# Chunked attention and two FFNs: token pairs of 512 and 384 columns, weight factors in two tiles, all attention weights transposed by TensorE

## The chip, the cores and the metric

The kernel runs on one core of one Trainium2 chip. The metric is the device time in microseconds (us) of one execution; less is better. TensorE (PE) multiplies, VectorE (DVE), ScalarE (ACT) and GpSimd (POOL) do the elementwise work, SyncE (SP) issues every DMA of this kernel. The weight loads of PE are shown as an engine of their own, PEld.

## The reference

Everything is float32. Attention works on chunks of 64 tokens; its output, 4608 tokens of 512 channels, goes through two feed-forward layers of 512 to 2048 to 512.

```python
scores = scale * np.matmul(q_c, k_c.transpose(0, 1, 2, 4, 3))   # chunks of 64, 8 batches, 8 heads, head size 64
scores = scores - np.max(scores, axis=-1, keepdims=True)
attn = np.exp(scores)
attn = attn / (np.sum(attn, axis=-1, keepdims=True) + 1e-09)
x = np.matmul(attn, v_c)                     # then put together as (4608, 512)
h = x @ w_in1
x = (h / (1.0 + np.exp(-1.702 * h))) @ w_out1
h = x @ w_in2
out = (np.maximum(h, 0.0) + alpha * np.minimum(h, 0.0)) @ w_out2
```

The weights arrive as 64-bit floats and are decoded on the chip by integer operations on VectorE.

## The kernel before, in words

Each float32 operand of a large product is split in a rounded part ("hi") and the rest ("lo"), and three matmuls (hi hi, hi lo, lo hi) make one product. A matmul has a stationary operand of 128x128, loaded by a weight load of its own, and a moving operand of up to 512 columns (tokens).

**First layer.** There are 9 blocks of 512 tokens and 16 slots f in each block, slot number n = 16 block + f. A slot runs `emit_h` (L446): 12 matmuls of 512 columns into a bank psH (there are two of them), a sigmoid on ACT (L460), then the work that `middle()` inserts, then the product g by DVE (L462), which frees the bank, and the split of g into gs by ACT (L117) and by DVE or POOL (L120). Then comes `emit_y` (L469) for the slot before last: 12 matmuls of 512 columns into the four psY. In slot 15 of a block x is split for the next block (`split_x`, L425). All engines run their own instructions in order, and the order is the order of the program text; nothing is reordered.

Attention of the later blocks is fitted between these. Each group g of 128 tokens from g = 4 on (four groups a block) has steps at half slots relative to 8 (g - 4): -4 `att_T` (transposes of q and k, L306), -1 `att_S` (scores, row maximum, difference, L332) and `att_E` (exponential on ACT, sum and reciprocal on DVE, the product e on POOL, L366), +2 `att_AT` (L372), +5 `att_PV` (product with v, two copies of x by ACT, L417). An even half slot is run in `middle()`, an odd one after `emit_y`. `att_AT` transposes e. Up to g = 7 TensorE does it, four transposes into a PSUM bank and one copy by ACT (L382, L387); from g = 8 on, 28 groups, DVE does it in 16 instructions of 32x128 each (L392). The banks come from `psum_att`, a pool of two that the scores, the transposes and the two banks of `att_PV` share in turn.

q and k of a group are loaded in 8 parts of several DMAs each (`load_qk`, L284), two groups ahead; v of the next group is loaded at half slot +5 into one of two buffers.

The second layer's weights are prepared in the same time, in 32 steps from slot 18 on, 3.25 slots apart (lists `todo`, key "prep"). A step, in slots from its base slot: +1 `prep_load` (raw weights), +2 `prep_abs` (Abs on ACT, L149), +3 `prep_decode` (four DVE operations), +4 `prep_store_a` (cast by ACT L222 and subtraction by POOL L223 into the tile "st2", store of 3 quarters by L205, then four sums on POOL), +6 `prep_store_b` (the same for the sums, into the same tile, all 4 quarters).

**Second layer.** Each matrix product is done with seven products of half-size blocks in place of eight. Tokens are taken in pairs: `PAIRS` has five entries, and a pair of n columns covers 2n tokens. For each pair there are four groups gr of hidden units; each has seven H products i in the order `H_ORDER`, of 2 x 6 matmuls of n columns each (L647), and seven Y products of 12 matmuls (L759) in `Y_ORDER`. H uses two bank pairs, psHa (i = 1, 6, 7, 4) and psHb (2, 5, 3); products are summed in the bank where they can be, and DVE and ACT take the rest (`h_after`, L674: copies, sums L692, `relus` L660, `leak` L665). Y uses psYa and psYb likewise and adds into `yacc` by DVE (L777) or ACT (L775).

The order is written by hand: a slot has one H product and one Y product of the group before, and a clock counts 1 for each half of an H product and 2 for a Y product. `at(when, ...)` puts work due at a clock value. `plan_group` (L721) sets when the Y operands are made: `op_hi` (ACT, L706), `op_lo` (DVE, L711), and the four differences (`diff`, L716, on POOL, in the last group on DVE). The first Y product comes when the first eight H products are done, so no Y product lies between the first group's H products. Weights are read from DRAM for every pair into rings of nine tiles (`load_wi`, L577) and four tiles (`load_wo`, L586), each reload issued when a tile has been used. `y_out` (L784) and, for the last pair, `y_last` (L799) transpose and store the output.

Of the kernel before, what the change touches and what calls it, by code (L numbers as in the profile page):

```python
# [9 lines left out]
F32 = mybir.dt.float32  # L10
# [23 lines left out]
PAIRS = (480, 480, 448, 448, 448)  # L34

H_ORDER = (1, 2, 6, 5, 7, 3, 4)
Y_ORDER = (1, 5, 6, 3, 7, 2, 4)
# [8 lines left out]
def tile_chunk_attention_two_ffn(  # L46
# [173 lines left out]
    def prep_split(step, src):  # L220
        t = prep_p.tile([P, 4, 2, P], F32R, tag="st2", name="st2")
        nc.scalar.copy(t[:, :, 0], src)  # L222
        nc.gpsimd.tensor_tensor(out=t[:, :, 1], in0=src, in1=t[:, :, 0].bitcast(F32), op=ALU.subtract)  # L223
        return t

    def prep_store_a(step):
        u = pr[step]
        t = prep_split(step, u)
        prep_store(step, 0, 3, t[:, 0:3])
        sums = dec_p.tile([P, 4, P], F32, tag="u", name="sums")  # L230
        a11, a12, a22, a21 = (u[:, q] for q in range(4))
        for o, x, y, op in (
            (0, a21, a22, ALU.add), (1, sums[:, 0], a11, ALU.subtract),
            (2, a11, a21, ALU.subtract), (3, a12, sums[:, 1], ALU.subtract),
        ):
            nc.gpsimd.tensor_tensor(out=sums[:, o], in0=x, in1=y, op=op)
        pr[step] = sums

    def prep_store_b(step):
        t = prep_split(step, pr.pop(step))  # L240
        prep_store(step, 3, 7, t)
# [20 lines left out]
    def load_qkv(g, names="qkv"):  # L262

        for nm in names:
            if g < GPB:
                t = {
                    "q": lambda: spare(f"wi{NF - GPB + g}", 0),
                    "k": lambda: spare(f"wi{NF - GPB + g}", 1),
                    "v": lambda: spare(f"wo{NF - 1 - g // 2}", g % 2),
                }[nm]()  # L270
            else:
                t = qkv_p.tile([P, 512], F32, tag=nm, name=nm, bufs=2)
# [99 lines left out]
    def att_AT(g):  # L372
# [5 lines left out]

        if g < 2 * GPB:
            ps = psum_att("psAT")  # L380
            for hp in range(HP):
                nc.tensor.transpose(  # L382
                    ps[:, hp * P:(hp + 1) * P],
                    e[:, 2 * hp:2 * hp + 2, :].rearrange("p u t -> p (u t)"),
                    ident,
                )
            nc.scalar.copy(t.rearrange("p h t -> p (h t)"), ps)  # L387
        else:
            blocks = e.rearrange("p (h c) (b e) -> p h c b e", c=2, e=SQ)
            for i in range(P // SQ):  # L390
                for o in range(P // SQ):
                    nc.vector.transpose(  # L392
                        t[o * SQ:(o + 1) * SQ, :, i * SQ:(i + 1) * SQ],
                        blocks[i * SQ:(i + 1) * SQ, :, o // 2, o % 2, :],
                    )
# [176 lines left out]
    hs = [(p, gr, i, jj) for p in range(NP) for gr in range(NGR) for i in H_ORDER for jj in range(2)]  # L572
# [22 lines left out]
    def second_layer():  # L595
# [125 lines left out]
        def plan_group(p, gr, u):  # L721

            n = PAIRS[p]
            last = (p, gr) == (NP - 1, NGR - 1)
            times = (23, 25, 27, 30, 35, 39, 43) if last else (27, 30, 34, 36, 44, 46, 49)
# [6 lines left out]
            t1, t2, t3, t4 = (24, 26, 29, 30) if last else (24, 32, 29, 38)  # L732
# [126 lines left out]
    with tc.manual_schedule():  # L859
# [50 lines left out]
        for i, step in enumerate(steps):  # L910
            n = PREP_FROM + int(i * PREP_EVERY)
            for lag, fn in enumerate((None, prep_load, prep_abs, prep_decode, prep_store_a, None, prep_store_b)):
                if fn:
                    todo.setdefault(("prep", n + lag), []).append(partial(fn, step))
# [3 lines left out]
        for g in range(GPB, NG):  # L918
# [3 lines left out]
            if g + 1 < NG:  # L922
                between[8 * (g - GPB) + 5].append((load_v, g + 1))
# [9 lines left out]
        for n in range(NBLK * NF):  # L933
# [14 lines left out]
            emit_h(n, middle, nc.gpsimd if ("decode", n) in todo else nc.vector)  # L948

# [60 lines left out]
```

## Time and profile before

| | us |
|---|---|
| three timed runs | 1734.43, 1737.24, 1738.43 |
| median | 1737.24 |
| the profiled execution's own time | 1733.37 |
| its span | 1731.6 |

The profile is of one execution. Rows of a timeline or chain give the start and the length, then engine, line and operation, out<-in by tile names, shapes and how many were merged (x12); a bracket gives the idle time before and what ended it. A merged matmul row also holds the last one's way through the array; the chain's lengths run to the next row's start.

### The profile page before, as it was taken

The page shows a single profiled execution, that of the slowest core. Times are in us where ns is not written, and L with a number is a line of the kernel's source. Part 1 is how long each engine was busy: PE and PEld are TensorE (multiplying, and loading weights), DVE is VectorE, ACT ScalarE, POOL GpSimd, SP SyncE. Part 2 cuts the span into 40 slices and gives each one's busy share as a digit, 9 for nine tenths or more (in the row PEclk, how much of TensorE's full clock was granted, in tenths as well). Part 3 has the DMA queues.
Part 4 walks back from the last instruction along what each step waited for, and adds up shares of the span by engine and source line. Part 5 has one row for each costly group of instructions (what it writes and reads, how often), then busy time and mean ns, then how long its engine had stood idle before and what let it go on. Part 6 is the DMA issues. An engine that isn't in the chain of part 4 may idle for free.

```text
span 1731.6 us, 25761 instructions
## 1 busy us (share of the span) xinstructions
PE 1631.3 (94%) x9257; PEld 1366.9 (79%) x9259; DVE 1267.8 (73%) x1858; ACT 785.2 (45%) x1098; POOL 500.4 (29%) x382
## 2 busy tenths in 40 slices
PE   7879998999988999989999989999999999999997
PEld 5667876777767777767788878888888998998996
DVE  7998666686666777757774347887788788788776
ACT  5554434344334443434433344555455455554542
POOL 3664122222212222212222024223422423422320
PEclk9999999999999999999999999999999999999999
DMA  8741334444334344334423067669667877977854
GB/s 229 215 115 36 73 88 110 114 109 111 93 92 107 107 110 115 101 97 118 100 62 125 0 214 249 203 180 293 214 204 194 309 217 193 313 212 192 278 180 121
DMA packets 388591, 268.11 MB, mean 155 GB/s; under 512 B 265840, under 2 KB 328048, under 8 KB 388464
## 3 DMA queue, kind: packets, MB, share of 16 engines
q1 hardware_dynamic: 388464, 266.47, 53.8%
q8 instruction: 73, 1.20, 0.3%
q14 instruction: 54, 0.44, 0.1%
HBM read 218.11 MB, written 48.23 MB: 154 GB/s over the span
## 4 chain that ended last, share of the span: by engine, by line
PE 45%; DVE 19%; DMA 8%; SPq 8%; ACT 7%; issue 4%; POOL 2%; DVEq 0%; ACTq 0%; POOLq 0%
PE psYa L759 10%; PE psHa L647 9%; PE psYb L759 7%; PE psHb L647 6%; SPq L297 6%; PE psH L453 6%; PE psY L476 5%; DMA raw<-in_moe_w_in_dram 3%; DMA raw<-in_moe_w_out_dram 3%; DVE g L462 2%; DVE g L666 2%; DVE at L392 2%; ACT gs L117 2%; DVE gs L120 1%; DVE o L711 1%
## 5 line engine op out<-in xcount | busy, mean ns | idle before, releaser
L453 PE MATMUL psH<-xs,wi 128*128 128x512 f32 x1728 | 442.7, 407 | 33.1 <-DVE g L462 29.5
L453 PEld LDWEIGHTS psH<-xs,wi 128*128 128x128 f32 x1728 | 330.6, 195 | 113.6 <-DVE g L462 37.8
L476 PE MATMUL psY<-gs,wo 128*128 128x512 f32 x1728 | 415.1, 390 | 3.6 <-ACT gs L117 3.6
L476 PEld LDWEIGHTS psY<-gs,wo 128*128 128x128 f32 x1728 | 323.7, 188 | 73.2 <-ACT gs L117 5.5
L117 ACT CAST gs<-g 128x512 fp32r<-128x512 f32 x144 | 89.3, 620 | 351.6 <-DVE g L462 351.6
L759 PE MATMUL psYa<-o,w 128*128 128x448 f32 (+1 forms) x960 | 218.6, 376 | 6.3 <-ACT o L706 3.8
L647 PE MATMUL psHa<-xop,wi2t 128*128 128x448 f32 (+1 forms) x960 | 216.0, 374 | 4.8 <-ACT g L663 4.4
L759 PEld LDWEIGHTS psYa<-o,w 128*128 128x128 f32 x960 | 180.2, 189 | 32.1 <-ACT o L706 5.1
L647 PEld LDWEIGHTS psHa<-xop,wi2t 128*128 128x128 f32 x960 | 181.7, 189 | 26.6 <-ACT g L663 4.8
L462 DVE TENSOR_TENSOR g<-psH,g 128x512 f32<-128x512 f32 x144 | 98.4, 683 | 138.5 <-ACT g L460 137.7
L666 DVE SCALAR_TENSOR_TENSOR g<-neg,minus_alpha,g 128x448 f32<-128x448 f32 (+1 forms) x160 | 182.7, 1182 | 6.8 <-ACT g L663 6.7
L759 PE MATMUL psYb<-o,w 128*128 128x448 f32 (+1 forms) x720 | 161.9, 373 | 0.0
L647 PE MATMUL psHb<-xop,wi2t 128*128 128x448 f32 (+1 forms) x720 | 160.1, 371 | 0.0
L120 DVE TENSOR_TENSOR gs<-g,gs 128x512 fp32r<-128x512 f32 x129 | 93.7, 726 | 88.6 <-ACT gs L117 87.9
L716 POOL TENSOR_TENSOR tsum<-g,tsum 128x896 f32<-128x896 f32 (+1 forms) x39 | 92.6, 2375 | 199.7 <-DVE o L711 196.9
L759 PEld LDWEIGHTS psYb<-o,w 128*128 128x128 f32 x720 | 134.8, 188 | 16.9 <-DVE o L711 0.6
L647 PEld LDWEIGHTS psHb<-xop,wi2t 128*128 128x128 f32 x720 | 135.2, 188 | 15.4
L716 POOL TENSOR_TENSOR tsum<-g,g 128x896 f32<-128x896 f32 (+1 forms) x19 | 41.6, 2188 | 350.9 <-DVE g L666 301.9
L392 DVE STREAM_TRANSPOSE at<-e 32x128 f32<-32x128 f32 x448 | 135.5, 302 | 6.7
L662 ACT ACTIVATE neg<-g 128x896 f32<-128x896 f32 (+1 forms) x60 | 58.5, 975 | 124.1 <-DVE g L692 124.1
L460 ACT ACTIVATE g<-psH 128x512 f32<-128x512 f32 x144 | 85.8, 596 | 50.7 <-PE psH L453 50.3
L711 DVE TENSOR_TENSOR o<-tsum,o 128x896 fp32r<-128x896 f32 (+1 forms) x60 | 66.5, 1109 | 46.1 <-ACT o L706 44.0
(117 smaller groups left out, 1898.8 us busy)
## 6 DMA issues: line engine op xcount, KB each, us to landing
wi2t<-wi SPq DMA_DIRECT2D x280, 256.0 KB, 3.8
w<-wo SPq DMA_DIRECT2D x140, 512.0 KB, 3.6
x<-ysb SPq DMA_DIRECT2D x36, 256.0 KB, 2.5
raw<-in_moe_w_in_dram SPq DMA_DIRECT2D x16, 512.0 KB, 5.4
raw<-in_moe_w_out_dram SPq DMA_DIRECT2D x16, 512.0 KB, 4.3
raw<-in_moe_w_in_dram SPq DMA_DIRECT2D x32, 256.0 KB, 3.9
wi<-st SPq DMA_DIRECT2D x16, 512.0 KB, 2.9
raw<-in_moe_w_out_dram SPq DMA_DIRECT2D x32, 256.0 KB, 3.5
```

The lines of the kernel that those rows point to most:

```text
L117: nc.scalar.copy(hi, src)
L120: eng_lo.tensor_tensor(out=lo, in0=src, in1=hi.bitcast(F32), op=ALU.subtract)
L297: nc.sync.dma_start(out=t[r:r + SQ, h // 2, off // SQ:(off + n) // SQ], in_=src[b, h, s:s + n, y * SQ:(y + 1) * SQ].rearrange("(b t) e -> ...
L392: nc.vector.transpose(t[o * SQ:(o + 1) * SQ, :, i * SQ:(i + 1) * SQ], blocks[i * SQ:(i + 1) * SQ, :, o // 2, o % 2, :],)
L453: nc.tensor.matmul(ps, w[:, a, c], xs[:, b, c], start=(i == 0), stop=(i == 3 * KT - 1))
L460: nc.scalar.activation(out=g, in_=ps, func=AF.Sigmoid, scale=1.702)
L462: nc.vector.tensor_tensor(out=g, in0=ps, in1=g, op=ALU.mult)
L476: nc.tensor.matmul(y_t[j][t], w[:, a, t * P:(t + 1) * P], gs[:, b], start=(f == 0 and a + b == 0), stop=(f == NF - 1 and b == 1),)
L647: nc.tensor.matmul(ps, w[:, c, a], x[b][:, c], start=(k == 0 and i in (1, 2, 5)), stop=(k == 5 and i in (2, 3, 4)), skip_group_check=True,)
L666: nc.vector.scalar_tensor_tensor(out=g, in0=neg, scalar=minus_alpha[:, f:f + 1], in1=g, op0=ALU.mult, op1=ALU.add)
L716: eng.tensor_tensor(out=wide(homes[out], n), in0=wide(homes[x], n), in1=wide(homes[y], n), op=ALU.subtract,)
L759: nc.tensor.matmul(ps[:, d, :n], w[:, jj, d, a], x[b][:, jj], start=(k == 0 and i in (1, 5, 2)), stop=(k == 5 and i in (3, 2, 4)), skip_gr ...
```

## The change

The pairs become three of 512 and two of 384 columns (2304 in all, as before). The first group (pair 0, gr 0) takes its H products in the order `H_FIRST`, with 4 before 3, and the last one in `H_LAST`, with 5 before 6 and 3 before 7; `plan_group` has other due times for the first, the last but one and the last group. The prepared factors go to two tiles, "sta" for 3 quarters and "stb" for 4, and the first cast and subtraction treat 3 quarters only; Abs is issued behind `emit_h` of the slot +3 (key "abs"), and `prep_store_b` at +5. TensorE transposes e for all groups. v has one buffer from g = 4 on, and its load stands at half slot +7.

```diff
--- before.py
+++ after.py
@@ -31,9 +31,12 @@
 PREP_FROM = 18
 PREP_EVERY = 3.25
 
-PAIRS = (480, 480, 448, 448, 448)
+PAIRS = (512, 512, 512, 384, 384)
 
 H_ORDER = (1, 2, 6, 5, 7, 3, 4)
+
+H_FIRST = (1, 2, 6, 5, 7, 4, 3)
+H_LAST = (1, 2, 5, 6, 3, 7, 4)
 Y_ORDER = (1, 5, 6, 3, 7, 2, 4)
 PLACE = {1: 0, 2: 1, 3: 6, 4: 2, 5: 3, 6: 4, 7: 5}
 
@@ -217,16 +220,15 @@
         except StopIteration as done:
             pr[step] = done.value[0].rearrange("p (q f) -> p q f", q=4)
 
-    def prep_split(step, src):
-        t = prep_p.tile([P, 4, 2, P], F32R, tag="st2", name="st2")
+    def prep_split(src, n, tag):
+        t = prep_p.tile([P, n, 2, P], F32R, tag=tag, name=tag)
         nc.scalar.copy(t[:, :, 0], src)
         nc.gpsimd.tensor_tensor(out=t[:, :, 1], in0=src, in1=t[:, :, 0].bitcast(F32), op=ALU.subtract)
         return t
 
     def prep_store_a(step):
         u = pr[step]
-        t = prep_split(step, u)
-        prep_store(step, 0, 3, t[:, 0:3])
+        prep_store(step, 0, 3, prep_split(u[:, 0:3], 3, "sta"))
         sums = dec_p.tile([P, 4, P], F32, tag="u", name="sums")
         a11, a12, a22, a21 = (u[:, q] for q in range(4))
         for o, x, y, op in (
@@ -237,8 +239,7 @@
         pr[step] = sums
 
     def prep_store_b(step):
-        t = prep_split(step, pr.pop(step))
-        prep_store(step, 3, 7, t)
+        prep_store(step, 3, 7, prep_split(pr.pop(step), 4, "stb"))
 
 
     def spans(t0, n):
@@ -269,7 +270,7 @@
                     "v": lambda: spare(f"wo{NF - 1 - g // 2}", g % 2),
                 }[nm]()
             else:
-                t = qkv_p.tile([P, 512], F32, tag=nm, name=nm, bufs=2)
+                t = qkv_p.tile([P, 512], F32, tag=nm, name=nm, bufs=1 if nm == "v" else 2)
             t = t.rearrange("p (h d) -> p h d", h=H)
             for off, n, b, s in spans(g * P, P):
                 nc.sync.dma_start(
@@ -375,24 +376,14 @@
             t = spare(f"wi{NF - GPB - 1 - g % 2}", 1).rearrange("p (h t) -> p h t", h=HP)
         else:
             t = at_p.tile([P, HP, P], F32, tag="at", name="at")
-
-        if g < 2 * GPB:
-            ps = psum_att("psAT")
-            for hp in range(HP):
-                nc.tensor.transpose(
-                    ps[:, hp * P:(hp + 1) * P],
-                    e[:, 2 * hp:2 * hp + 2, :].rearrange("p u t -> p (u t)"),
-                    ident,
-                )
-            nc.scalar.copy(t.rearrange("p h t -> p (h t)"), ps)
-        else:
-            blocks = e.rearrange("p (h c) (b e) -> p h c b e", c=2, e=SQ)
-            for i in range(P // SQ):
-                for o in range(P // SQ):
-                    nc.vector.transpose(
-                        t[o * SQ:(o + 1) * SQ, :, i * SQ:(i + 1) * SQ],
-                        blocks[i * SQ:(i + 1) * SQ, :, o // 2, o % 2, :],
-                    )
+        ps = psum_att("psAT")
+        for hp in range(HP):
+            nc.tensor.transpose(
+                ps[:, hp * P:(hp + 1) * P],
+                e[:, 2 * hp:2 * hp + 2, :].rearrange("p u t -> p (u t)"),
+                ident,
+            )
+        nc.scalar.copy(t.rearrange("p h t -> p (h t)"), ps)
         at_t[g] = t
 
     x_t = {}
@@ -569,7 +560,12 @@
 
 
 
-    hs = [(p, gr, i, jj) for p in range(NP) for gr in range(NGR) for i in H_ORDER for jj in range(2)]
+    FIRST_G, LAST_G = (0, 0), (NP - 1, NGR - 1)
+    h_order = {FIRST_G: H_FIRST, LAST_G: H_LAST}
+    hs = [
+        (p, gr, i, jj) for p in range(NP) for gr in range(NGR)
+        for i in h_order.get((p, gr), H_ORDER) for jj in range(2)
+    ]
     ys = [(p, gr, i) for p in range(NP) for gr in range(NGR) for i in Y_ORDER]
     wi_order, wo_order, wi_q, wo_q = list(hs), list(ys), [], []
     turn = {"wi": 0, "wo": 0}
@@ -721,15 +717,20 @@
         def plan_group(p, gr, u):
 
             n = PAIRS[p]
-            last = (p, gr) == (NP - 1, NGR - 1)
-            times = (23, 25, 27, 30, 35, 39, 43) if last else (27, 30, 34, 36, 44, 46, 49)
+            last = (p, gr) == LAST_G
+            times = {
+                FIRST_G: (27, 31, 36, 37, 44, 46, 49), LAST_G: (23, 22, 26, 28, 34, 38, 42),
+                (NP - 1, NGR - 2): (27, 30, 34, 33, 44, 46, 40),
+            }.get((p, gr), (27, 30, 34, 36, 44, 46, 49))
             for i, nm, hi in zip(
                 (1, 5, 6, 3, 7, 2, 4), ("g11", "t", "t", "g22", "t3", "g21", "t"), times
             ):
                 at(u + hi, op_hi, p, gr, i, nm)
                 at(u + hi + 1, op_lo, p, gr, i, nm)
             eng = nc.vector if last else nc.gpsimd
-            t1, t2, t3, t4 = (24, 26, 29, 30) if last else (24, 32, 29, 38)
+            t1, t2, t3, t4 = {FIRST_G: (28, 34, 30, 38), LAST_G: (20, 24, 28, 29)}.get(
+                (p, gr), (24, 32, 29, 38)
+            )
             at(u + t1, diff, n, "t", "g12", "g11", eng)
             at(u + t2, diff, n, "t", "g22", "t", eng)
             at(u + t3, diff, n, "t3", "g22", "g12", eng)
@@ -909,9 +910,11 @@
         ]
         for i, step in enumerate(steps):
             n = PREP_FROM + int(i * PREP_EVERY)
-            for lag, fn in enumerate((None, prep_load, prep_abs, prep_decode, prep_store_a, None, prep_store_b)):
-                if fn:
-                    todo.setdefault(("prep", n + lag), []).append(partial(fn, step))
+            for what, lag, fn in (
+                ("prep", 1, prep_load), ("abs", 3, prep_abs), ("prep", 3, prep_decode),
+                ("prep", 4, prep_store_a), ("prep", 5, prep_store_b),
+            ):
+                todo.setdefault((what, n + lag), []).append(partial(fn, step))
 
 
         between = {}
@@ -920,7 +923,7 @@
                 if g > GPB or at > 0:
                     between.setdefault(8 * (g - GPB) + at, []).append((fn, g))
             if g + 1 < NG:
-                between[8 * (g - GPB) + 5].append((load_v, g + 1))
+                between.setdefault(8 * (g - GPB) + 7, []).append((load_v, g + 1))
             if g + 2 < NG:
                 for part in range(8):
                     between.setdefault(max(0, 8 * (g - GPB) - 1 + part), []).append(
@@ -946,6 +949,8 @@
                 dec = ahead
 
             emit_h(n, middle, nc.gpsimd if ("decode", n) in todo else nc.vector)
+            for fn in todo.get(("abs", n), []):
+                fn()
 
 
             ahead_y = {0: (n - 1,), 1: (), NF - 1: (n - 2, n - 1)}.get(f, (n - 2,))
```

## Rows read from the trace of the kernel before

**Rows 1.** the page's first line: span and instruction count

```profile
span 1731.6 us, 25761 instructions
```

**Rows 2.** chain in order of time, first layer: start us, us, what

```profile
162.09 2.95 PE psH L453 x12
176.54 2.95 PE psH L453 x12
200.46 2.95 PE psH L453 x12
...
907.97 2.72 PE psH L453 x12
```

**Rows 3.** waits, 162 to 908 us: who waited for whom, us, times, longest

```profile
ACT u L149 <- DMA raw<-in_moe_w_in_dram: 41.5, 13, 6.0
ACT u L149 <- DMA raw<-in_moe_w_out_dram: 41.1, 14, 5.0
PEld psH L453 <- DVE g L462: 25.4, 24, 4.0
PEld psS L340 <- ACT x L417: 18.1, 11, 4.1
PEld psX L409 <- DVE at L392: 16.0, 18, 2.3
ACT st L222 <- DMA wi<-st: 9.1, 4, 6.1
```

**Rows 4.** timeline of ACT and PE, 494 to 526 us: start, us, what

```profile
504.07 0.66 ACT L149 ACTIVATE u<-raw 128x512 f32<-128x512 f32 x1 [5.97 <-DMA raw<-in_moe_w_in_dram]
520.60 0.62 ACT L222 CAST st<-u 128x512 fp32r<-128x512 f32 x1 [6.09 <-DMA wi<-st]
...
523.91 2.45 PE L453 MATMUL psH<-xs,wi 128*128 128x512 f32 x5 [3.24 <-DVE g L462]
```

**Rows 5.** groups by line, attention's transposes: busy us, mean ns | idle before

```profile
L392 DVE STREAM_TRANSPOSE at<-e 32x128 f32<-32x128 f32 x448 | 135.5, 302 | 6.7
L387 ACT COPY at<-psAT 128x512 f32<-128x512 f32 x4 | 2.3, 574 | 0.0
```

**Rows 6.** timeline of PE's weight loads at 138 us, four transposes by TensorE

```profile
138.50 0.56 PEld L382 LDWEIGHTS psAT<-ident,e 128*128 128x128 f32 x4
```

**Rows 7.** timeline of PE and POOL at 515 us

```profile
515.07 2.88 PE L453 MATMUL psH<-xs,wi 128*128 128x512 f32 x12
...
515.81 1.05 POOL L366 TENSOR_TENSOR e<-e,d 128x512 f32<-128x512 f32 x1 [6.55 <-DVE d L365]
```

**Rows 8.** chain in order of time: matmuls of 512, 480 and 448 columns

```profile
989.57 8.16 PE psY L476 x36
1033.89 2.62 PE psYb L759 x12
1036.52 2.59 PE psHb L647 x12
...
1706.14 2.48 PE psYb L759 x12
1716.93 2.44 PE psYb L759 x12
```

**Rows 9.** timeline of weight loads after a pause; their group by line

```profile
1460.67 0.30 PEld L759 LDWEIGHTS psYa<-o,w 128*128 128x128 f32 x2 [0.80 <-DVE o L711]
...
L759 PEld LDWEIGHTS psYa<-o,w 128*128 128x128 f32 x960 | 180.2, 189 | 32.1 <-ACT o L706 5.1 <-DVE o L711 4.2 <-issue 1.2
```

**Rows 10.** timelines of PE and DVE at the second layer's start and end

```profile
1021.05 5.01 PE L647 MATMUL psHa<-xop,wi2t 128*128 128x480 f32 x12 [4.43 <-ACT g L663]
...
1702.15 3.99 PE L759 MATMUL psYa<-o,w 128*128 128x448 f32 x12 [3.84 <-ACT o L706]
...
1700.90 1.15 DVE L777 TENSOR_TENSOR yacc<-psYa,yacc 128x448 f32<-128x448 f32 x2
```

**Rows 11.** busy us by stretch: PE, PEld, DVE, ACT, POOL; clock, DMA share, GB/s

```profile
1454.00:1489.00 35.00, 34.24 (x166) 30.76 (x165) 26.52 (x29) 17.61 (x20) 11.11 (x6) 1.00 0.92 258
```

## The prediction

> **What bounds the kernel now.** I read the page first: the span is 1731.6 us [rows 1] and the profiled execution took 1733.37 us. The median of the three timed runs, 1737.24, lies 3.9 us above it. Then the chain in order of time splits the span. In the first layer the reader is to see an undisturbed stretch: a psH group starts at 176.54 and the one four slots later at 200.46, so four slots with one attention group in them take 23.92 us [rows 2]. Sixteen slots (a block) should then take 95.7 us and seven blocks 669.8 us. The seven blocks from 162.09 to 907.97 took 745.9 us [rows 2]. So TensorE, in order, loses 76 us there, and the waits name the losses [rows 3]: psH for VectorE's L462 25.4, scores for ScalarE's copies of x 18.1, the attention's product psX for VectorE's transposes L392 16.0, some 60 us of the 76. I put most of the rest down to the halved clock that follows such pauses.
>
> Two waits of ScalarE stand behind the first two of these. Its Abs of the second layer's raw weights (L149) waits 82.6 us for their load, and its cast into the tile "st2" (L222) waits for the store of the tile's earlier content [rows 3]. In [rows 4] one of each is seen, 5.97 and 6.09 us, and psH stands still for 3.24 us at 523.91, just behind the second.
>
> In the second layer TensorE is nearly gapless, so the time of one matmul counts. The rows give 8.16 us for 36 of 512 columns, 226.7 ns each; 2.62 and 2.59 us for 12 of 480, about 217; 2.48 and 2.44 us for 12 of 448, 206.7 and 203.3 [rows 8]. I take 205 for 448. Two pauses stand out: 4.43 us after the first group, then 12 matmuls in 5.01 us instead of 2.6, as at the lower clock level, 1.2 GHz, and 3.84 us ahead of the last group's products, then 3.99 instead of 2.48 [rows 10].
>
> **The change, part by part.**
>
> *Transposes.* For 28 groups it removes 448 VectorE transposes, 135.5 us [rows 5], and adds 112 TensorE transposes and 28 ScalarE copies at 574 ns, 16.1 us of ScalarE. The four transposes of an earlier group held the weight loads for 0.56 us [rows 6]; part of that lies under the matmuls around it, so I take 0.5 us a group, 14 us on the path. The wait for L392 goes whole: the copy now follows TensorE directly and the product comes three half slots later. TensorE now waits for e itself, in order, with the next psY group queued behind. In [rows 7] GpSimd ends e at 516.86 and TensorE ends the matmuls ahead of the transposes at 517.8, so I cost this wait at nothing, 0.9 us being the cover. VectorE's L462 no longer queues behind 4.8 us of transposes. Late next would be the block boundary, where L462 queues behind the split of x.
>
> *Abs, two tiles, v.* Abs moves from the end of a slot to behind the next slot's gs cast, about half a slot of two 2.72 us groups later, and behind one more sigmoid, so a wait of 6 us at most [rows 3] should shrink to little. The load of raw weights keeps its place on SP's queue. Two tiles let a cast run while the other tile's store is out. The first cast and subtraction lose a quarter of their columns, off the path. The b store moves a slot earlier on SP, and may hold the next q and k loads, which are two groups ahead. With one buffer for v, its load, moved two half slots later, waits for the product of the group before; queued behind on SP are q and k pieces and the raw loads. No row prices it: between nothing and half a slot now and then. I take nothing, because the v is needed six half slots later.
>
> Together: the 16.0 us go. Of the 43.5 us of the other two waits I take half, 22, because the block boundary and SP's many small loads remain. With some 6 us of half clock this removes 44. The bounds are the 16 alone and all 76. Net of 14: 30 us gained, between 2 and 62.
>
> *Columns.* The number of matmuls and the sum of columns stay; only their split moves. A pair is 672 matmuls (4 groups, 7 products, 24 each). Before: 1344 at 217.5 and 2016 at 205 ns, 705.6 us. After: 2016 at 226.7, 457.0 us, and 1344 of 384 columns, which no row shows. Over the stream itself (columns at 2.4 GHz, the full level) the rows leave 13.4 ns at 512, 17.5 at 480, 18.3 at 448. For 384, 160 ns of stream, I take 19, as at 448, the nearest: 179 ns, 240.6 us. That is 697.6, 8 us less. The lower bound is 13.4 ns over the stream, 173.4 ns, 16 us less; the upper bound is no gain over 448, 205 ns, 275.5 us, 27 us more. A constant cost per matmul would make the split worth exactly nothing, since columns and count are unchanged; what the 8 us rest on is that 512 pays least. The Trainium skill, "TensorE: Matmul & The Clock Gate", section "Back-to-back issue gap", has such a constant, columns at 2.4 GHz plus 2.5 ns; by it the term is 0. The rows' 13.4 to 18.3 ns are larger and not constant, so I go by them, and keep 0 as a rival.
>
> *First and last group.* In the first group product 4 comes before 3, so ScalarE's two passes over bank a run beside product 3's 2.7 us. New is that 4 follows 7 in the same bank and waits for VectorE's addition; the bank's addition of the last group, 1.15 us [rows 10], is the nearest row, so 1.5 us with the way there and back. Of 4.43 plus the 2.4 us of slow matmuls, 5 go (bounds 2 and 7). At the end, bank psYa came free only with VectorE's addition ending at 1702.05 [rows 10], queued behind the last group's differences. The new order and times issue these some clock steps earlier; what stays is the addition itself, 1.15 us. Of 3.84 plus 1.5 us I take 4 (bounds 0 and 5). The other shifted times of the last but one group I cost at nothing, hidden by TensorE's row of products.
>
> *Sum.* 1733.4 - 30 - 8 - 5 - 4 = 1686.4 for an execution like the profiled one. The median stands 3.9 above; taking half of that, I say 1688.
>
> **Rivals.**
>
> *Constant cost per matmul.* As above: 1696.
>
> *Weight transfers.* Each pair reads the same weights, and shorter pairs read them faster. One stretch of 35 us, about a group of 448 columns, has a DMA share of 0.92, 32.2 us of transfers [rows 11]; a 384 group (168 matmuls at 179 ns) is 30 us. Nine and four tiles of read-ahead, over half a group, cover one such stretch. Where they do not, each group waits 2.2 us, in the four groups of a pair 9 us: 1697.
>
> *No relief in the first layer.* SP's many loads or the block boundary take up what VectorE and ScalarE give. Only the 16 us go, against 14: 1716. For it speaks that the raw load is late because of SP, which is not relieved; against it that Abs is given half a slot.
>
> *384 no faster than 448.* If a matmul cannot follow a weight load faster than now, the price is 205 ns: 35 us over my forecast, 1723. Against it: after a pause two weight loads lie in 0.30 us, where one takes 189 ns on average [rows 9], so the second began some 0.11 us after the first, and 160 ns leave room. The Trainium skill, same page, section "LDWEIGHTS (loading the stationary operand)", gives columns over 1.2, 107 ns for 128; the trace's 0.11 us agrees.
>
> *Slower: TensorE waits for e.* The transposes stand in TensorE's own queue, ahead of the psY group. With stalls gone TensorE reaches them sooner, while e's way (maximum, exponential, sum, product on three engines) does not shorten. The price is 28 times the wait. It decides from 49 us over my forecast, 1.75 us a group; at 2.2 us a group it gives 62 more, 1750. Against it is the 0.9 us to spare at a stalled place [rows 7].
>
> **How the numbers follow.** My forecast 0.45, constant cost 0.12, transfers 0.06, no relief 0.17, flat 384 0.11, waits for e 0.09. The likeliest gives 1688. Downward, all of the 76 less some, with the lower column bound, reaches 1664; upward the range takes in no relief and a little of flat 384, to 1722. A measurement of this kernel tells about 0.2%, 3.5 us, from no change. The slower cases are waits for e, and flat 384 without relief, 1751: 0.10. Between, 0.03. Faster 0.87.
>
> **What would show it.** The blocks of the first layer at 98 to 103 us instead of 106.6; no L392; psX's wait gone; L149's wait for raw below 30 us; no L222 wait; four transposes holding 0.5 us a group; psAT's wait for e below 10 us in all. In the second layer 12 matmuls of 512 in 2.72 us and of 384 in 2.08 to 2.2; the first pause about 1.5 us, the last about 1.2. The prediction is wrong if 12 of 384 take 2.4 us, if psAT waits over 1 us a group, or if blocks stay above 105 us.

## Result and profile after

The changed kernel takes 1690.78 us (median of four runs, 1689.83 to 1691.14), beside 1737.84 for the kernel before in the same comparison (four runs; the table ahead has three of them). The ratio is 0.973 with an interval of 0.971 to 0.975: 2.7% faster. The forecast was 1688 in a range of 1664 to 1722. The profiled execution took 1690.86 us; its span follows, where [rows 1] had 1731.6.

```profile
span 1689.1 us, 25576 instructions
```

Two stretches split the span, and I use them for every run below. **Seven blocks** run from the first psH group of the second block to that of the ninth: 745.8 us before, 705.0 after. The **second layer** runs from its first matmul to the end: 734.0 before (997.6 to 1731.6), 733.3 after (955.7 to 1689.1). So nearly all of the gain of the span (42.5 us) lies in the first layer, 40.8 where 30 were forecast, and the second layer gave 0.7 where 17 were. The stretches are those of one profiled execution of each kernel.

**First layer.** From the chain in order of time, as in [rows 2]; start and length in us:

```profile
176.00 2.95 PE psH L444 x12
...
200.42 2.95 PE psH L444 x12
```

Four undisturbed slots now take 24.42 us instead of 23.92. The half microsecond is the four transposes on TensorE; the weight loads of one such group, from PE's timeline as in [rows 6], and ScalarE's copies, from the groups by line as in [rows 5]:

```profile
190.75 0.59 PEld L381 LDWEIGHTS psAT<-ident,e 128*128 128x128 f32 x4
```

```profile
L386 ACT COPY at<-psAT 128x512 f32<-128x512 f32 x32 | 18.6, 582 | 0.0
```

Twenty-eight groups of 24.42 us are 684 us, so of the seven blocks 21 us are pauses. Before it was 76 (745.8 less 669.8). The waits of the seven blocks, as in [rows 3]: who waited for whom, us in total, times, longest:

```profile
ACT u L152 <- DMA raw<-in_moe_w_in_dram: 32.0, 7, 11.8
ACT u L152 <- DMA raw<-in_moe_w_out_dram: 23.6, 6, 10.6
...
PEld psS L341 <- ACT x L408: 12.3, 5, 4.4
...
PE psS L341 <- ACT x L408: 10.2, 3, 4.0
...
PE psX L400 <- DMA v<-in_v_dram: 3.8, 2, 2.1
```

The waits for VectorE's L392, for the stores of "st2" and of psH for L462 are gone. ScalarE's wait for raw weights is 55.6 us in 13 waits, where it was 82.6 in 27; there are fewer, but the longest is now 11.8 us, where it was 6.0. TensorE itself waits 14.0 us, 10.2 for the copies of x and 3.8 for v; the rest of the 21 goes mostly with slow matmuls behind these waits (a psH group of 4.61 us instead of 2.88 at 500.91). What such a wait does is seen in the timelines of SP, ScalarE and TensorE at 282 us:

```profile
277.45 1.53 SPq L202 DMA_DIRECT2D raw<-in_moe_w_in_dram  x2
...
282.40 0.66 ACT L152 ACTIVATE u<-raw 128x512 f32<-128x512 f32 x1 [9.99 <-DMA raw<-in_moe_w_in_dram]
282.96 0.64 ACT L408 COPY x<-psX 128x256 f32<-128x256 f32 x2
...
283.37 1.92 PE L341 MATMUL psS<-kT,qT 64*64 64x64 f32 x32 [4.02 <-ACT x L408]
```

SP issues the load only at 277.45, when ScalarE has already stood at its Abs for 5 of the 9.99 us; from 262 us on SP had issued 29 other DMAs one after another, 22 of them small loads of q and k. The copies of x are behind it in its queue, the scores need the banks that these copies free, and TensorE stands 4.02 us at the scores. Two more such stretches have waits of TensorE of 1.72 and 3.94 us (500 and 512 us) and of 2.08 and 2.27 us (729 and 740 us). The first of each is put down to the load of v, which now has one buffer, the second to the copies of x. They come every 36 slots, where a group spans two batches and its q and k come in twice as many DMAs on SP.

**Second layer.** Three runs of 12 matmuls of 384 columns from PE's timeline (their starts are 2.08 us apart):

```profile
1667.54 2.24 PE L760 MATMUL psYa<-o,w 128*128 128x384 f32 x12
...
1669.62 2.24 PE L760 MATMUL psYb<-o,w 128*128 128x384 f32 x12
...
1671.70 2.24 PE L760 MATMUL psYa<-o,w 128*128 128x384 f32 x12
```

Over all matmuls of the second layer I took the distance from one start to the next, and counted what lies over 60 ns above the usual one of its shape as a pause (a slow matmul at the lower clock level counts there too). Pairs overlap in time, so up to 1 us of a pair's pauses can go to its neighbour; the sums are firm. The usual distance, the mean of those without a pause, is 227.5 ns at 512 columns, 217.6 at 480, 204.8 at 448, 174.2 at 384. The pauses, us in each pair:

| | pair 0 | 1 | 2 | 3 | 4 | sum |
|---|---|---|---|---|---|---|
| before | 7.5 | 1.3 | 1.5 | 1.5 | 7.9 | 19.7 |
| after | 4.2 | 2.1 | 2.7 | 10.9 | 11.2 | 31.1 |

The matmuls themselves fell by 12.5 us (1344 x 217.6 + 2016 x 204.8 = 705.3 us; 2016 x 227.5 + 1344 x 174.2 = 692.8). The pauses rose by 11.4, nearly all in the two pairs of 384 columns. PE's timeline at the worst place:

```profile
1456.03 1.31 PE L643 MATMUL psHa<-xop,wi2t 128*128 128x384 f32 x6 [0.48 <-DMA wi2t<-wi]
...
1462.06 1.34 PE L643 MATMUL psHb<-xop,wi2t 128*128 128x384 f32 x6 [1.57 <-DMA wi2t<-wi]
1465.98 2.26 PE L760 MATMUL psYa<-o,w 128*128 128x384 f32 x6 [2.58 <-DMA w<-wo]
```

The weights come late. What SP issues in that time, from its timeline:

```profile
1438.99 5.73 SPq L795 DMA_DIRECT2D out_dram<-x_t  x8
1444.82 0.93 SPq L588 DMA_DIRECT2D w<-wo  x2
1445.84 6.01 SPq L795 DMA_DIRECT2D out_dram<-x_b  x8
1451.95 0.93 SPq L579 DMA_DIRECT2D wi2t<-wi  x2
1452.98 5.60 SPq L795 DMA_DIRECT2D out_dram<-x_t  x8
```

The output of the pair before goes out in bursts of eight stores, 5.6 to 6.0 us each, and the weight loads stand between them. The busy times by stretch, as in [rows 11], show a lower mean granted clock (0.91) and DMA engines that are nearly full (0.96):

```profile
1440.00:1480.00 40.00, 35.21 (x184) 33.96 (x184) 24.91 (x30) 17.34 (x24) 8.54 (x5) 0.91 0.96 287
```

At the start, where [rows 10] had one pause of 4.43 us, three short ones are left, and ahead of the last group's products 2.60 where 3.84 were; but among the last group's H products two new ones have come, 0.88 us at 1636.62 and the one at 1654.13:

```profile
970.93 3.03 PE L643 MATMUL psHa<-xop,wi2t 128*128 128x512 f32 x12 [1.39 <-DVE g L688]
983.35 2.81 PE L760 MATMUL psYa<-o,w 128*128 128x512 f32 x11 [0.97 <-DVE o L707]
986.66 3.04 PE L643 MATMUL psHa<-xop,wi2t 128*128 128x512 f32 x12 [0.49 <-ACT g L685]
...
1654.13 2.38 PE L643 MATMUL psHa<-xop,wi2t 128*128 128x384 f32 x12 [0.55 <-DVE g L688]
...
1663.30 2.32 PE L760 MATMUL psYa<-o,w 128*128 128x384 f32 x12 [2.60 <-issue]
```

### The profile page after: what moved, and what is told of

Read it like the earlier page. It is cut to its first block, busy times and chain, and to the rows that moved or that the text cites. A ratio compares the mean times of both kernels' runs of the same rounds, so it can differ in the third digit from the quotient of the medians.

```text
span 1689.1 us, 25576 instructions
## 1 busy us (share of the span) xinstructions
PE 1622.5 (96%) x9371; PEld 1353.3 (80%) x9371; DVE 1111.7 (66%) x1410; ACT 801.6 (47%) x1126; POOL 490.9 (29%) x382
## 2 busy tenths in 40 slices
DMA packets 385580, 268.09 MB, mean 159 GB/s; under 512 B 265648, under 2 KB 323504, under 8 KB 385456
## 4 chain that ended last, share of the span: by engine, by line
PE 68%; DVE 11%; SPq 5%; DMA 3%; issue 3%; ACT 3%; POOL 0%; DVEq 0%; ACTq 0%; POOLq 0%
PE psH L444 18%; PE psY L467 18%; PE psHa L643 8%; PE psYa L760 8%; PE psYb L760 6%; PE psHb L643 5%; SPq L298 4%; DVE g L662 3%; DVE o L707 2%; DVE yacc L778 2%; PE psS L341 2%; DVE g L688 1%; PE psX L400 1%; DMA raw<-in_moe_w_in_dram 1%; DVE xop L556 1%
## 5 line engine op out<-in xcount | busy, mean ns | idle before, releaser
L760 PE MATMUL psYa<-o,w 128*128 128x512 f32 (+1 forms) x960 | 218.0, 373 | 11.1 <-DMA w<-wo 4.0
L643 PE MATMUL psHa<-xop,wi2t 128*128 128x512 f32 (+1 forms) x960 | 212.4, 370 | 3.0 <-DVE g L688 1.9
L760 PEld LDWEIGHTS psYa<-o,w 128*128 128x128 f32 x960 | 175.3, 189 | 41.8 <-DVE o L707 10.8
L662 DVE SCALAR_TENSOR_TENSOR g<-neg,minus_alpha,g 128x512 f32<-128x512 f32 (+1 forms) x160 | 178.7, 1158 | 9.9 <-ACT g L659 9.7
L643 PE MATMUL psHb<-xop,wi2t 128*128 128x512 f32 (+1 forms) x720 | 158.8, 369 | 3.3 <-DMA wi2t<-wi 2.5
L760 PE MATMUL psYb<-o,w 128*128 128x512 f32 (+1 forms) x720 | 159.1, 368 | 0.3 <-DVE o L707 0.3
L712 POOL TENSOR_TENSOR tsum<-g,tsum 128x1024 f32<-128x1024 f32 (+1 forms) x39 | 93.0, 2385 | 188.6 <-DVE o L707 188.6
L712 POOL TENSOR_TENSOR tsum<-g,g 128x1024 f32<-128x1024 f32 (+1 forms) x19 | 42.6, 2243 | 361.5 <-DVE g L662 311.4
L367 POOL TENSOR_TENSOR e<-e,d 128x512 f32<-128x512 f32 x32 | 33.4, 1045 | 300.5 <-DVE d L366 273.9
L658 ACT ACTIVATE neg<-g 128x1024 f32<-128x1024 f32 (+1 forms) x60 | 58.6, 976 | 122.5 <-DVE g L688 122.5
L707 DVE TENSOR_TENSOR o<-tsum,o 128x1024 fp32r<-128x1024 f32 (+1 forms) x60 | 66.5, 1109 | 40.5 <-ACT o L702 40.4
```

Source lines behind the costliest of these rows:

```text
L643: nc.tensor.matmul(ps, w[:, c, a], x[b][:, c], start=(k == 0 and i in (1, 2, 5)), stop=(k == 5 and i in (2, 3, 4)), skip_group_check=True,)
L662: nc.vector.scalar_tensor_tensor(out=g, in0=neg, scalar=minus_alpha[:, f:f + 1], in1=g, op0=ALU.mult, op1=ALU.add)
L707: nc.vector.tensor_tensor(out=lo, in0=wide(homes[nm], n), in1=hi.bitcast(F32), op=ALU.subtract)
L712: eng.tensor_tensor(out=wide(homes[out], n), in0=wide(homes[x], n), in1=wide(homes[y], n), op=ALU.subtract,)
L760: nc.tensor.matmul(ps[:, d, :n], w[:, jj, d, a], x[b][:, jj], start=(k == 0 and i in (1, 5, 2)), stop=(k == 5 and i in (3, 2, 4)), skip_gr ...
```

## Experiments

Twelve kernels ran. Each ratio is to the kernel before as it ran on the same chip; that kernel's medians are 1732.9 us (e1 to e4), 1735.0 (e5 to e8) and 1733.2 (e12 to e15), beside 1737.8 in the result's comparison, so ratios of different sets compare to about 0.3%. The stretches come from one profile each. Kernels that share a stretch show how far it repeats: the changed first layer (after, e4, e5, e13, e14) takes 701.8 to 706.7 us in the seven blocks, the changed second layer (after, e6, e7, e8, e15) 731.4 to 737.2. So a difference within 5 or 6 us between two single profiles does not count by itself.

| | ratio, 95% interval | seven blocks | second layer | pauses in it |
|---|---|---|---|---|
| before | 1 | 745.8 | 734.0 | 19.7 |
| after | 0.973 (0.971 to 0.975) | 705.0 | 733.3 | 31.1 |
| e1 transposes alone | 0.984 (0.982 to 0.985) | 719.1 | 735.0 | 21.5 |
| e2 preparation alone | 0.975 (0.973 to 0.976) | 703.4 | 735.1 | 20.3 |
| e3 pairs alone | 1.002 (1.001 to 1.004) | 744.5 | 738.4 | 36.8 |
| e4 after, pairs undone | 0.973 (0.971 to 0.975) | 704.8 | 729.6 | 16.0 |
| e5 after, stores by ScalarE | 1.015 (1.013 to 1.017) | 706.2 | 801.9 | 99.6 |
| e6 after, raw loads by ScalarE | 0.967 (0.965 to 0.969) | 689.3 | 737.2 | 35.1 |
| e7 e6 with VectorE's transposes | 0.960 (0.957 to 0.963) | 681.4 | 731.4 | 29.3 |
| e8 after, Abs undone | 0.978 (0.976 to 0.980) | 711.1 | 735.1 | 32.9 |
| e12 e7 with the old pairs | 0.961 (0.959 to 0.963) | 683.2 | 733.6 | 19.7 |
| e13 after, orders undone | 0.979 (0.978 to 0.981) | 706.7 | 737.5 | 35.5 |
| e14 after, stores spread | 0.972 (0.970 to 0.974) | 701.8 | 725.7 | 23.8 |
| e15 after, one tile | 0.977 (0.975 to 0.978) | 705.4 | 734.5 | 32.4 |

### The parts one by one: e1 to e4

e1 is the kernel before with the change's `att_AT` alone.

```diff
-        if g < 2 * GPB:
-            ps = psum_att("psAT")
...
-        else:
-            blocks = e.rearrange("p (h c) (b e) -> p h c b e", c=2, e=SQ)
...
+        ps = psum_att("psAT")
```

> The kernel before with one edit: TensorE transposes e for all groups. The first layer's seven blocks went from 745.9 to 705.0 us with the whole change, and 14 us of new transposes are in that, so 55 us of pauses went. Theory 1 (the late raw loads and the shared tile are the root, VectorE's transposes only the occasion): transposes alone take away the 16 us wait for L392 and a few us of the wait for L462 and cost 14: 1729 to 1735 us, blocks together 737 to 743. Theory 2 (VectorE's load is the root): most of the 55 us goes with the transposes alone: 1700 to 1715 us, blocks together 710 to 722.

Measured: 1706.17 us, seven blocks 719.1 us, 26.7 less, both in theory 2's ranges. The wait for raw weights did not fall, it rose from 82.6 to 112.5 us:

```profile
ACT u L149 <- DMA raw<-in_moe_w_in_dram: 58.5, 13, 9.8
ACT u L149 <- DMA raw<-in_moe_w_out_dram: 54.0, 13, 8.9
```

So the gain is not a relief of that wait. One reading, not tested by itself, is that the other engines reach a slot sooner while the load still comes when SP comes to it. That VectorE's load is a cause of its own, as theory 2 has it, is not ruled out by this run.

e2 is the kernel before with two tiles, the Abs' new place, the earlier second store and v in one buffer; VectorE transposes as before.

```diff
-        t = prep_p.tile([P, 4, 2, P], F32R, tag="st2", name="st2")
+        t = prep_p.tile([P, n, 2, P], F32R, tag=tag, name=tag)
...
+                ("prep", 1, prep_load), ("abs", 3, prep_abs), ("prep", 3, prep_decode),
+                ("prep", 4, prep_store_a), ("prep", 5, prep_store_b),
```

> The kernel before with the preparation's edits alone: two tiles for the factors, Abs behind the next slot's H group, the second store a slot earlier, one buffer for v (the tiles' room comes from it). Theory 1 (late raw loads and the shared tile are the root): 30 to 40 us of pauses go, 1698 to 1708 us, and the psH wait for L462 falls below 12 us though VectorE still transposes. Theory 2 (VectorE's load is the root): at most 15 us go, 1723 to 1733 us; ScalarE's waits shrink, but psH still waits for L462 some 20 us and psX for L392 16 us.

Measured: 1690.52 us, seven blocks 703.4, 42.4 less, as much as the whole change and beyond theory 1's range. The waits of its seven blocks:

```profile
ACT u L149 <- DMA raw<-in_moe_w_in_dram: 14.3, 5, 7.2
...
ACT u L149 <- DMA raw<-in_moe_w_out_dram: 12.5, 5, 7.6
...
PE psX L407 <- DMA v<-in_v_dram: 6.3, 3, 2.6
...
PEld psX L407 <- DVE at L390: 3.9, 8, 0.6
...
PEld psH L451 <- DVE g L460: 1.7, 8, 0.4
```

The wait for VectorE's transposes fell from 16.0 to 3.9 us, and that of psH for VectorE's product from 25.4 to 1.7, without any transpose being moved. A wait for v is new, as in the kernel after. So e1 and e2 do not add: 26.7 and 42.4 alone, 40.8 together, and neither theory holds alone.

e3 is the kernel before with the new pairs, e4 the kernel after with the old ones.

```diff
-PAIRS = (480, 480, 448, 448, 448)
+PAIRS = (512, 512, 512, 384, 384)
```

> The kernel before with one edit: pairs of 512, 512, 512, 384, 384. By the two profiles matmuls of the second layer take 12 us less with them (705.4 to 693.1), while its stretch is only 0.8 us shorter. Theory 1 (the short pairs bring their own pauses, weights late behind the output's stores): 12 less, some 8 to 10 back, 1733 to 1737 us, with TensorE waiting for wi2t and w in the first group of pairs 4 and 5. Theory 2 (the pauses come from the new orders and due times): the full 12 us, 1724 to 1727 us.

> The changed kernel with the pairs of before (480, 480, 448, 448, 448), all else as changed. Theory 1 (short pairs bring pauses that take back what the columns give): within 4 us of the changed kernel, 1689 to 1695 us, and no wait of TensorE for wi2t or w above 1 us after the first group. Theory 2 (columns give 12 us, pauses come from the orders and times): 1700 to 1704 us.

Measured: with the new pairs the second layer is 4.4 us longer in e3 than before, and 3.7 us longer after than in e4. In the timed runs e3 (1735.55 us) is 0.2% slower than before, and e4 and after have the same ratio; e4's 1686.28 us lies 3 us under theory 1's range. In both theory 1 is the nearer. Pairs of 512 and 384 are worth nothing here, or a little less. In e3 as in after the pauses are in pairs 3 and 4 (9.3 and 14.5 us), in e4 they are not (1.2 and 7.5).

### What is behind the late raw weights: e6, e7, e8, e15

e6 lets ScalarE issue the loads of raw weights, at the same place of the program.

```diff
-            nc.sync.dma_start(out=raw[:, 1:3] if b else raw[:, 0:4:3], in_=src[:, b])
+            nc.scalar.dma_start(out=raw[:, 1:3] if b else raw[:, 0:4:3], in_=src[:, b])
```

> The changed kernel, with the raw weights of the preparation (2 loads a step) issued by ScalarE in place of SP, at the same place of the program. The first layer's seven blocks take 705.0 us, 21 above 28 groups of 24.43. Theory 1 (the raw load is late because it stands behind q and k loads on SP): ScalarE's wait for raw falls from 56 us below 15, blocks 688 to 693, 12 to 17 us less. Theory 2 (what is late is something else, the score's or v's own loads on SP, or the transfers themselves): blocks 700 to 706, within 5 us.

Measured: seven blocks 689.3, 15.7 us less than after, and 5.3 over 28 undisturbed groups (684): theory 1. No wait of Abs for raw weights is left; the one wait of ScalarE that the rows still put down to them is this, at the sigmoid:

```profile
ACT g L451 <- DMA raw<-in_moe_w_in_dram: 9.6, 3, 3.4
```

The loads were late because SP came late to them, as at 277.45 us in the timeline of after, not because the DMA engines were slow.

e7 is e6 with the old `att_AT`, 28 groups by VectorE.

> As the run with the raw loads on ScalarE, with VectorE's transposes of before for the 28 groups. The transposes alone and the preparation alone took 27 and 42 us off the seven blocks, both together 41. Theory 1 (the transposes helped only because VectorE came out of the pauses late; without late raw loads they cost their 14 us and save the 16 us wait for L392): blocks within 4 us of those of the run with TensorE's transposes. Theory 2 (VectorE's load still makes pauses of its own): 8 us or more longer. Theory 3 (with no late loads VectorE's transposes hide): 8 us or more shorter, near 682.

Measured: 681.4 us, 7.9 less than e6 (theory 3), and 0.960 of the kernel before, with e12 the fastest that ran; the ratios of e6 and e7 were taken on one chip and their intervals do not meet. 28 groups without the transposes on TensorE would take 669.8. So the path is rid of 14.2 us and gets 6.3 back as waits. With the raw weights in time, transposing on TensorE is a loss. What still stops TensorE here is mostly v, not the transposes, for which TensorE waits 1.6 us:

```profile
PE psX L409 <- DMA v<-in_v_dram: 5.8, 2, 3.3
```

e8 is the kernel after with the Abs at the end of the slot +2.

```diff
-                ("prep", 1, prep_load), ("abs", 3, prep_abs), ("prep", 3, prep_decode),
+                ("prep", 1, prep_load), ("prep", 2, prep_abs), ("prep", 3, prep_decode),
```

> The changed kernel with Abs back at the end of the slot before (its place in the kernel before); two tiles, second store and v stay as changed. Theory 1 (Abs's place is what the preparation's gain comes from): ScalarE waits 80 us or more for raw, blocks 718 to 728 us, 13 to 23 us longer. Theory 2 (the two tiles are): blocks 705 to 710.

Measured: 711.1 us, 6.1 more than after, in none of the two ranges, but just above theory 2's. The wait for raw weights is back at 88.8 us, as theory 1 said, but it costs less than that theory had. A wait that neither the kernel before nor the one after had appears, of the product for the copy of the transposed attention weights:

```profile
PEld psX L400 <- ACT at L386: 13.2, 2, 6.7
```

e15 is the kernel after with both stores through one tile of four quarters, the second at +6.

```diff
-        prep_store(step, 0, 3, prep_split(u[:, 0:3], 3, "sta"))
+        t = prep_split(step, u)
+        prep_store(step, 0, 3, t[:, 0:3])
...
-                ("prep", 4, prep_store_a), ("prep", 5, prep_store_b),
+                ("prep", 4, prep_store_a), ("prep", 6, prep_store_b),
```

> The kernel after, with both stores of a preparation step through one tile again, four quarters in the first cast, and the second store a slot later as before. Theory 1 (the store's hold on the tile was the larger part of the preparation's gain): seven blocks 720 to 730 us, up from 705, waits of ScalarE's cast for the tile's store of 9 us or more again, ratio 0.982 to 0.988. Theory 2 (the tile's wait was short in sum, 9.1 us with four long ones, and the Abs' place was the gain): seven blocks 706 to 712 us, ratio 0.973 to 0.978.

Measured: 705.4 us, the same as after. ScalarE waits for the tile 37.5 us in 20 waits, and for raw weights less than after:

```profile
ACT u L152 <- DMA raw<-in_moe_w_in_dram: 28.2, 7, 6.8
ACT u L152 <- DMA raw<-in_moe_w_out_dram: 20.9, 7, 6.9
ACT st L225 <- DMA wi<-st: 20.8, 11, 7.9
ACT st L225 <- DMA wo<-st: 16.7, 9, 7.9
```

Theory 2 is nearer: the blocks came out just under its range, the ratio inside it. The second tile is worth nothing that shows beside the other parts: from e1 (719.1) the Abs' place with the change of v takes 13.7 us (e15), two tiles and the earlier second store with the change of v 8.0 (e8), and all of it 14.1 (after). The change of v was not run by itself.

### Why the second layer gave nothing: e5, e13, e14

e5 lets ScalarE issue the output's stores.

```diff
-                    nc.sync.dma_start(
+                    nc.scalar.dma_start(
                         out=out[t0:t0 + n, c:c + SQ].rearrange("(b i) e -> i b e", i=SQ),
```

> The changed kernel, with the output's 32 stores of a pair issued by ScalarE in place of SP. In the changed kernel TensorE's pauses in the second layer sum to 31 us (20 before), most of the new ones in the first groups of the 384 pairs, where SP issues 8 stores in some 5.6 us between two rounds of weight loads. Theory 1 (SP's issue time holds the weight loads): the waits for wi2t and w of pairs 4 and 5 go, second layer 733 to some 724 us, 8 to 10 us less in all, if ScalarE's own work is not held. Theory 2 (the DMA engines are full there, share 0.95): the waits stay within 2 us, the second layer at 731 to 736 us.

Measured: the second layer grew by 68.6 us, which no theory had. From the waits of its second layer:

```profile
DVE o L707 <- ACT o L702: 113.6, 35, 8.9
ACT o L702 <- DMA out_dram<-x_b: 37.3, 4, 9.5
PEld psYa L760 <- ACT o L702: 35.0, 12, 4.3
```

ScalarE is held while its stores are issued, and VectorE and TensorE wait for its casts. No wait of TensorE for wi2t or w is left, but with TensorE this much slower that decides nothing. What it shows is that a burst of eight stores holds the engine that issues it.

e13 is the kernel after with the H order, due times and differences of before in the first and the last groups.

```diff
-H_FIRST = (1, 2, 6, 5, 7, 4, 3)
-H_LAST = (1, 2, 5, 6, 3, 7, 4)
+H_FIRST = H_ORDER
+H_LAST = H_ORDER
```

> The kernel after, with the first and last group's H order and all due times and differences of before. Theory 1 (orders and due times took the pauses of the first and last group): the second layer grows from 733.3 to 737 to 739 us, with 4.4 us ahead of the second group's first products back, and some 3.8 us ahead of the last group's; ratio to the kernel before 0.975 to 0.977. Theory 2 (those pauses went because of the 512 and 384 columns, not because of the orders): second layer 732 to 735 us, ratio 0.972 to 0.974.

Measured: second layer 737.5 us, 4.2 more, in theory 1's range but hardly above the 737.2 of e6 (the ratio came out above both ranges; the seven blocks were 1.7 us longer as well). Both pauses are back, from PE's timeline:

```profile
981.56 4.55 PE L643 MATMUL psHa<-xop,wi2t 128*128 128x512 f32 x12 [4.67 <-ACT g L659]
...
1667.83 3.75 PE L759 MATMUL psYa<-o,w 128*128 128x384 f32 x12 [3.86 <-ACT o L702]
```

The kernels together tell more than this one. With old pairs and old orders the second layer takes 734.0, 735.0 and 735.1 us (before, e1, e2); with new pairs and old orders 738.4 and 737.5 (e3, e13); with old pairs and new orders 729.6 and 733.6 (e4, e12); with both new 731.4 to 737.2, 734.3 in the mean. By the means the pairs cost about 3 us and the orders give 3 to 4, and so the layer stayed where it was; single profiles would not show this.

e14 is the kernel after with the eight stores of a quarter of the output issued one per clock step.

```diff
+            def store(d, a):
...
             for d in range(2):
                 for a in range(P // SQ):
-                    c = half * 2 * P + d * P + a * SQ
-                    nc.sync.dma_start(
...
+                    at(clock + 1 + 4 * d + a, store, d, a)
```

> The kernel after, with the eight stores of each output quarter issued one per clock step over eight steps, still by SyncE, in place of eight in a row (4.2 to 6.0 us of SyncE's queue each). Theory 1 (weight loads of the 384 pairs are late because they queue behind eight stores): the pauses of the second layer fall from 31 us to 20 to 24, the second layer from 733.3 to 724 to 728 us, ratio 0.967 to 0.970. Theory 2 (the DMA engines' own share of 0.95, or SyncE's total work, is what binds the 384 groups): pauses stay at 28 to 34 us, second layer 731 to 736, ratio 0.972 to 0.975.

Measured: second layer 725.7 us, 7.6 less, and below all five kernels with the second layer of after (731.4 to 737.2); 7.3 us fewer pauses. Both are as by theory 1. The ratio missed theory 1's range and lies at the lower edge of theory 2's, but it is 0.4% below e15's on the same chip, whose second layer is that of after. TensorE's waits for weights in the second layer, first of after, then of e14, in which none for wi2t is left:

```profile
PE psYa L760 <- DMA w<-wo: 4.0, 2, 2.6
...
PE psHb L643 <- DMA wi2t<-wi: 2.5, 2, 1.6
...
PE psHa L643 <- DMA wi2t<-wi: 0.5, 1, 0.5
```

```profile
PE psYa L760 <- DMA w<-wo: 1.7, 1, 1.7
```

The one that is left is at the worst place, and the stretch shows the DMA engines full:

```profile
1467.99 2.32 PE L760 MATMUL psYa<-o,w 128*128 128x384 f32 x12 [1.70 <-DMA w<-wo]
```

```profile
1440.00:1480.00 40.00, 37.94 (x214) 36.78 (x213) 28.30 (x35) 21.73 (x30) 9.80 (x5) 1.00 1.00 284
```

A DMA share of 1.00 points to the transfers themselves as what is next. It is not shown: no run took bytes away, and e4 moved 317 GB/s at a share of 0.93 from 1420 to 1460 us, with TensorE busy throughout, so 284 GB/s is not the most that the engines move.

### A faster version: e12

e12 is e7 with the old pairs.

> The kernel after with three parts undone or altered at once: ScalarE issues the loads of raw weights (as in e6), VectorE transposes e again from g = 8 on (as in e7), and the pairs are the old 480 and 448. Theory 1 (the two losses are independent: transposes by TensorE some 8 to 11 us, pairs of 512 and 384 some 4 us): seven blocks 681 us as in e7, second layer 728 us, ratio to the kernel before 0.957 to 0.959. Theory 2 (the 4 us of the pairs were a shift of pauses that another timing gives back): no better than e7, ratio 0.960 to 0.962.

Measured: 0.961, as e7; theory 2. In the second layer (733.6 us, e7 731.4) the matmuls lost what the pauses gave back (19.7 instead of 29.3 us). e7's changes with e14's stores were not run together; that each would keep most of its gain, since they lie in different layers, is an estimate.

## Why the prediction was right, and where not

The time came within 3 us of the forecast, and was made of two misses of opposite sign: 10.8 us more than forecast in the first layer, 16.3 less in the second. That they nearly cancel is luck; that the first layer's pauses would be the gain was right.

**The first layer was undersized.** The step that fell short is the 44 us that I let go of the 76, half of the two waits behind ScalarE and VectorE. It measured 55 (76 to 21). The price was right: 24.42 instead of 23.92 us in four slots, 0.50 us a group, 14 in all. TensorE's wait for e, the slower rival, did not come: no wait of psAT for e shows in the seven blocks.

**The 16 us of the transposes were put down to the wrong part.** The prediction let this wait go because the transposes leave VectorE. e2 shows it fall to 3.9 us with the transposes in place. That fits one queue of waits, as the timeline at 282 us shows it for the scores: the load late, so Abs, so the copies of x, so the banks. If the waits are links of one chain, relief at more than one link can take the same microseconds, and the parts' gains overlap, as those of e1 and e2 do. For L392 this chain is argued from the rows and not tested by itself. e7 shows that the transposes' own worth is negative, 8 us, once raw is in time.

**The raw load keeps its place on SP.** I wrote so, and then expected its wait below 30 us; it was 55.6. By e6, SP's queue is the cause, and 15.7 us were still to be had there. What moving the load alone would give the kernel before was not run.

**v's one buffer.** The term was put at nothing, because v is needed late. TensorE waits 3.8 us for v after, 6.3 in e2 and 5.8 in e7; the kernel before has no such wait.

**Columns.** The term was 8 us and measured 12.5, since 384 columns pay 14.2 ns over the stream, as 512 do, and not 19. The Trainium skill, "TensorE: Matmul & The Clock Gate", section "Back-to-back issue gap", has one constant for all sizes, which it gives for an isolated matmul; by it the split would give nothing. It is not the distance in this stream of weight loads and matmuls, as the section itself warns for such streams. The measured distances have 14.2 ns over the stream at 512 and 384, and 17.6 and 18.1 at 480 and 448; so the split is not neutral.

**What took the columns' gain.** The rival "weight transfers" came in part, beside the forecast. It was priced at 9 us, the four groups of one pair, though two pairs are of 384; pairs 3 and 4 have 22.1 us of pauses where 9.4 were, 12.7 more. But the cause is only in part the one I gave. e14 takes away 7.3 us of pauses with the same 268.09 MB moved, so over half was SP's queue, with the stores in it. The prediction's price had counted transfers and left out the time that SP takes to issue the stores. The rest may be the transfers (share 1.00); no run took bytes away.

**First and last group.** 5 and 4 us were forecast. Pair 0 gave 3.3, and in e13, with the old orders, its 4.67 us pause is back. The last group gave next to nothing, 7.1 to 6.6 us: what was won ahead of its Y products went to the new pauses among its H products. Of the pause of 2.60 us the profile names no cause ("issue"); it ends 0.1 us after VectorE's second addition out of bank psYa does, at 1663.19:

```profile
1662.18 1.01 DVE L778 TENSOR_TENSOR yacc<-psYa,yacc 128x384 f32<-128x384 f32 x2
```

The weights had landed and ScalarE's cast had ended by 1662.2, so this fits the wait for the bank that the prediction priced at 1.15 us, with VectorE's addition out of psYb and its L662 ahead of the addition; it was not tested.

## What to carry to other kernels

Waits that stand behind one another in one in-order engine can be one loss: look for the earliest of them, here a DMA that is late in its issuer's queue, and price that one; the gains of parts that touch the others need not add (26.7 and 42.4 us alone, 40.8 together). Count the issue time of each queue in the stretch where reads get denser, stores included, before trusting a gain in matmul time. And when a part is right only because another engine is late, test it again after that is mended.

## What was unexpected of the hardware

The time of a matmul over its column stream is not smooth in the columns: 14.2 ns at 512, 17.6 at 480, 18.1 at 448, 14.2 at 384. Eight stores of 64 KB hold SP's queue 4.2 to 6.0 us, and when ScalarE issues them (e5) its casts come up to 9.5 us late.
